# Second matmul of an MLP turned round: columns of D on the partitions, 512 tokens wide, results turned by DMA transposes

## Chip, cores, metric

One core of a Trainium2 chip. The metric is the device time of one execution in microseconds (us). All runs told here were in the fast state, except three of the four executions of x_act, which is said there; the medians are over four to six executions of a changed kernel and three to eleven of the kernel before.

## The reference

```python
B, S, D, F = 1, 2048, 1024, 3584          # x, w1, b1, w2, b2 in bf16
def reference(x, w1, b1, w2, b2):
    y = _layernorm(x, axis=-1)
    h = _gelu(jnp.einsum("bsd,df->bsf", y, w1) + b1)      # first matmul
    return jnp.einsum("bsf,fd->bsd", h, w2) + b2          # second matmul
```

## The kernel before

Both matmuls are done by the Strassen-Winograd scheme on two levels: an outer scheme of 7 products replaces 8, and each of these is again 7 inner products. VectorE forms the sums of inputs and outputs, ScalarE copies partial sums between PSUM and SBUF, TensorE does the products. In the code `p` is the outer product, `q` the inner one, `u, v` the quarter of the result, `dt` (after) a tile of 128 columns of D. In stage 2 the last outer product is `p = 3`.

The kernel plans itself while it is built: it gives every instruction a cost from a small table, schedules it, and places the buffers by a search with a random `SEED`. Its order of DMA issues thus depends on what it believes a DMA costs.

Before, h is the stationary operand. A product is 14 matmuls of 256 columns, tokens come out on the partitions, and a result needs one addition and one store:

```python
def finish(b, i, k, u, v, a, na, bb, nb, name, t0=0, nt=2, q="SP"):
    o = M.alloc(nt * 512, "o")
    ...
    op("DVE", 0.08 + n / 960, lambda e: e.tensor_tensor(out=v16(o, 0, 2 * n, BF16), in0=a, in1=bb, op=ALU.add),
       r=[na, nb], w=[o.c()], name=name, lat=D_PS_LAT)
    store(b, i, k, u, v, o, t0, nt, q)          # rows of 512 B straight to the output

def prod2(b, p):
    ...
            for t in ts:                        # two tiles of 128 tokens
                for k in range(KQ):             # KQ = 7
                    i = e.matmul(bank2(bank)[:, t, :], lhsT=av3[:, k, t * P:(t + 1) * P], rhs=bv[:, k, :], ...)

c_seq = [("c", b, p) for p in P_ORDER for b in range(NB)]     # the two token halves one after the other
```

## Time and profile before

| | before |
|---|---|
| median (range), 3 runs | 334.92 us (334.42 to 335.51) |
| span of the profiled execution | 332.0 us |
| first matmul of 512 columns / first matmul of stage 2 / last matmul ends | 16.26 / 177.05 / 329.43 us |
| tail, from the last matmul to the end | 2.57 us |

The span is what the core itself records; the time of the same execution is 1.7 us longer. I cut the span into four: head (up to 16.26), stage 1 (to 177.05), stage 2 (to 329.43), tail. Before, TensorE is busy without a gap in the middle two, and the chain, the groups and some stretches that show it stand in the prediction. From the view of busy time by stretches of the kernel before (stretch, then busy us and count of PE, weight loads, VectorE, ScalarE, GpSimd, then clock, DMA share, GB/s):

```profile
300.00:320.00 20.00, 20.00 (x186) 17.93 (x184) 16.37 (x24) 4.07 (x7) 0.00 (x0) 1.00 0.73 206
320.00:332.00 12.00, 9.42 (x87) 8.19 (x84) 6.30 (x10) 0.59 (x1) 0.00 (x0) 1.00 0.26 77
```

At the end each of the last two stores lands (its completion is signalled) 1.6 us after its issue, the last at 331.5. The span ends 0.5 us after that.

### The profile page before, as it was taken

What the parts mean: (1) busy time and instruction counts of PE and PEld (TensorE: products, weight loads), DVE (VectorE), ACT (ScalarE), POOL (GpSimd) and SP (SyncE); (2) the same over time, 40 slices, a digit from 0 to 9 for tenths busy, and PEclk for the clock granted to TensorE, in tenths of its full rate; (3) what the DMA queues carried; (4) which work ended last, traced back from release to release, by engine and by line L of the source; (5) the groups of instructions that cost most, each with busy time, mean ns of one, the idle gap of its engine ahead of it and who ended that gap; (6) DMA issues with size and microseconds to landing.
All of it is one profiled execution on the core that took longest, in us unless ns stands there. A gap on an engine that the chain in (4) does not pass through costs nothing.

```text
span 332.0 us, 6015 instructions
## 1 busy us (share of the span) xinstructions
PE 328.2 (99%) x2328; PEld 220.2 (66%) x2328; DVE 297.8 (90%) x483; ACT 180.3 (54%) x307; POOL 12.7 (4%) x28
## 2 busy tenths in 40 slices
PE   8999999999999999999999999999999999999996
PEld 5944444444444444444447888888888888888885
DVE  5989999999999969977889995899999999999935
ACT  4697999899676776767765555533021222222020
POOL 2210021002000000000000000000000000000000
PEclk9999999999999999999999999999999999999999
DMA  8996899999997999999949462654856547569732
GB/s 233 324 242 189 276 249 335 260 320 290 300 337 258 345 330 310 317 355 300 283 142 305 132 204 71 198 146 136 238 162 188 163 126 206 177 165 266 199 109 79
DMA packets 103622, 76.88 MB, mean 232 GB/s; under 512 B 16426, under 2 KB 94890, under 8 KB 103594
## 3 DMA queue, kind: packets, MB, share of 16 engines
q1 hardware_dynamic: 103034, 76.18, 78.2%
q8 instruction: 18, 0.29, 0.4%
q10 hardware_dynamic: 560, 0.33, 0.3%
q14 instruction: 10, 0.08, 0.1%
HBM read 48.96 MB, written 24.38 MB: 221 GB/s over the span
## 4 chain that ended last, share of the span: by engine, by line
PE 97%; DMA 2%; SPq 1%; DVE 0%; issue 0%
PE ps L908 49%; PE ps L1175 45%; PE ps L1238 2%; DMA mem<-in_w_dram 2%; PE ps L705 0%; SPq L644 0%; SPq L772 0%; DVE mem L1095 0%; SPq L641 0%; PE ps L1197 0%; PE ps L1250 0%
## 5 line engine op out<-in xcount | busy, mean ns | idle before, releaser
L908 PE MATMUL ps<-mem 128*128 128x512 f16 x756 | 164.0, 379 | 0.0
L1175 PE MATMUL ps<-mem 128*128 128x256 f16 (+1 forms) x1372 | 150.4, 273 | 0.0
L1175 PEld LDWEIGHTS ps<-mem 128*128 128x128 f16 x1372 | 134.2, 98 | 16.4
L908 PEld LDWEIGHTS ps<-mem 128*128 128x128 f16 (+1 forms) x756 | 73.7, 98 | 88.6 <-ACT mem L838 0.9
L838 ACT COPY mem<-ps 128x512 f32<-128x512 f32 x111 | 64.7, 588 | 76.6 <-PE ps L1175 59.3
L822 ACT ACTIVATE mem<-ps,b_sb 128x512 f16<-128x512 f32 x112 | 73.9, 692 | 21.4 <-PE ps L908 14.7
L846 DVE TENSOR_TENSOR ps<-ps,mem 128x512 f32<-128x512 f32 x84 | 58.4, 695 | 17.4 <-ACT mem L838 15.1
L1065 DVE TENSOR_TENSOR mem<-mem 128x1792 f16<-128x1792 f16 x56 | 60.1, 1085 | 3.5 <-PE ps L1175 2.7
L783 DVE TENSOR_TENSOR mem<-mem 128x1024 f16<-128x1024 bf16 (+1 forms) x56 | 37.8, 686 | 1.0 <-DMA mem<-in_w_dram 0.7
L974 DVE TENSOR_TENSOR mem<-mem 128x512 f16<-128x512 f16 (+5 forms) x84 | 37.4, 463 | 0.8 <-DMA mem<-in_w_dram 0.2
L1076 DVE TENSOR_TENSOR mem<-mem 128x1792 f16<-128x1792 f16 x32 | 33.8, 1085 | 0.1
L829 ACT COPY ps<-ps 128x512 f32<-128x512 f32 x31 | 17.7, 570 | 27.4 <-PE ps L1175 25.2
L1095 DVE TENSOR_TENSOR mem<-ps,mem 128x512 bf16<-128x512 f32 (+1 forms) x25 | 16.4, 666 | 2.2 <-PE ps L1175 2.0
L958 DVE TENSOR_TENSOR mem<-mem 128x2048 f16<-128x2048 bf16 (+1 forms) x16 | 17.4, 1087 | 0.1
L669 DVE BATCH_NORM_STATS2 st_sb<-mem 128x6 f32<-128x512 bf16 x22 | 14.2, 680 | 3.4 <-DMA mem<-in_x_dram 3.4
L1108 DVE TENSOR_TENSOR mem<-ps,mem 128x512 f32<-128x512 f32 x24 | 16.1, 684 | 0.0
L749 DVE TENSOR_TENSOR mem<-mem 128x512 f16<-128x512 f16 x32 | 11.9, 418 | 0.2
L675 POOL TENSOR_TENSOR rstd_sb<-vpe_sb,nhalf 128x1 f32<-128x1 f32 x11 | 6.6, 598 | 48.0 <-DVE vpe_sb L672 48.0
L1197 PE MATMUL ps<-ones 128*128 128x128 bf16 (+1 forms) x55 | 6.7, 287 | 1.1 <-POOL ones L610 1.1
L1238 PE MATMUL ps<-mem 128*128 128x128 f16 x112 | 7.4, 219 | 0.1
L678 DVE TENSOR_SCALAR mem<-mem,mv_sb,rstd_sb 128x1024 f16<-128x1024 bf16 (+1 forms) x12 | 6.1, 519 | 0.9 <-POOL rstd_sb L675 0.7
L651 ACT ACTIVATE mem<-mem 128x1024 f16<-128x1024 bf16 x5 | 5.3, 1069 | 2.8 <-DMA mem<-in_x_dram 2.8
(33 smaller groups left out, 62.5 us busy)
## 6 DMA issues: line engine op xcount, KB each, us to landing
mem<-in_w_dram SPq DMA_DIRECT2D x80, 256.0 KB, 5.0
mem<-w_scr SPq DMA_DIRECT2D x28, 448.0 KB, 3.7
w_scr<-mem SPq DMA_DIRECT2D x21, 512.0 KB, 5.5
w_raw<-mem SPq DMA_DIRECT2D x12, 512.0 KB, 5.0
mem<-w_raw SPq DMA_DIRECT2D x12, 448.0 KB, 4.3
mem<-in_w_dram SPq DMA_DIRECT2D x9, 448.0 KB, 4.5
mem<-in_x_dram SPq DMA_DIRECT2D x15, 256.0 KB, 4.1
out_dram<-mem SPq DMA_DIRECT2D x30, 128.0 KB, 3.2
```

What stands on the lines that cost most here:

```text
L783: op("DVE", d_tt(n), lambda e: e.tensor_tensor(out=o[0], in0=a[0], in1=bb[0], op=f), r=[a[1], bb[1]], w=[o[1]], name=f"w1S{k}_{ch}")
L822: op("ACT", A_GELU, lambda e: e.activation(out=dst, in_=bank2(bank), func=ACT.Gelu_apprx_tanh, bias=b1_sb[:, f:f + 1], scale=1.0), r=[bank ...
L829: op("ACT", A_CP, lambda e: e.copy(out=banks[dst][:, :], in_=banks[src][:, :]), r=[bank_c[src]], w=[bank_c[dst]], name=name, lat=A_LAT)
L838: op("ACT", A_CP, lambda e: e.copy(out=v16(a, 0, 2048, F32), in_=banks[src][:, :]), r=[bank_c[src]], w=[a.c()], name=name, lat=A_LAT)
L846: op("DVE", D_PS, lambda e: e.tensor_tensor(out=banks[dst][:, :], in0=banks[src][:, :], in1=v16(a, 0, 2048, F32), op=ALU.add), r=[bank_c[s ...
L908: i = e.matmul(banks[bank][:, :], lhsT=lv[:, k, :], rhs=rv[:, k, :], start=(fresh and k == 0), stop=(k == KH - 1), skip_group_check=True)
L958: op("DVE", d_tt(2 * self.n), lambda e: e.tensor_tensor(out=vd, in0=va, in1=vb, op=ALU.subtract), r=self.cells(a) + self.cells(bb), w=self ...
L974: tt = lambda o, a, c: (lambda e: e.tensor_tensor(out=o, in0=a, in1=c, op=ALU.subtract))
L1065: op("DVE", d_tt(UN // 2), lambda e: e.tensor_tensor(out=v16(t), in0=a[0], in1=bb[0], op=f), r=a[1] + bb[1], w=[t.c()], name=f"in{b}_{p}{q}")
L1076: op("DVE", d_tt(UN // 2), lambda e, va=va, vb=vb, vd=vd: e.tensor_tensor(out=vd, in0=va, in1=vb, op=f), r=h_cells(b, a, u, s) + h_cells(b ...
L1095: op("DVE", 0.08 + n / 960, lambda e: e.tensor_tensor(out=v16(o, 0, 2 * n, BF16), in0=a, in1=bb, op=ALU.add), r=[na, nb], w=[o.c()], name= ...
L1175: i = e.matmul(bank2(bank)[:, t, :], lhsT=av3[:, k, t * P:(t + 1) * P], rhs=bv[:, k, :], start=(fresh and t == ts[0] and k == 0), stop=(t ...
```

## The change

Intent: 512-column matmuls pay TensorE's fixed cost per instruction half as often. So w2 becomes the stationary operand, 512 tokens stream through, and D comes out on the partitions. The two column tiles run in lockstep, so that each w2 unit and each sum of inputs serves both. The price: a result has to be turned before it is stored. The core of the diff:

```diff
-            def finish(b, i, k, u, v, a, na, bb, nb, name, t0=0, nt=2, q="SP"):
+            def finish(dt, i, k, u, v, a, na, bb, nb, name, alone=False, q="SP"):
+                o = M.alloc(1024, "o")
+                wait = 1.0 if q == "ACTQ" else FIN_DUE
+                op("DVE", D_PS, lambda e: e.tensor_tensor(out=v16(o, 0, 1024, BF16), in0=a, in1=bb, op=ALU.add), ...)
+                view = v16(t, 0, 2048, BF16).rearrange("p (t c) -> p t c", t=4)   # t: one buffer for both column tiles
+                half = view[:, :, dt * P:(dt + 1) * P]
+                dma("SP", lambda e: e.dma_start_transpose(half, v16(o, 0, 1024, BF16)), [o.c()], [t.c(dt)], P * 1024 * 1.3, None, f"To{key}")
+                if alone:
+                    store(i, k, u, v, half, [t.c(dt)], dt * P, P, q=q)
+                elif len(t.cells) == 2:                                           # both tiles turned
+                    store(i, k, u, v, view, [t.c(0), t.c(1)], 0, 2 * P, q=q)
...
+                    # last two products: their partial sum, split in f16 hi and lo, is turned; the product comes out by tokens
+                    dma("SP", lambda e: e.dma_start_transpose(v3(tt, 0, 2048, 8), v16(hl)), [hl.c(0), hl.c(1)], [tt.c()], P * 2048 * 1.3, None, f"Td{n}")
...
-                        for t in ts:
-                            for k in range(KQ):
-                                i = e.matmul(bank2(bank)[:, t, :], lhsT=av3[:, k, t * P:(t + 1) * P], rhs=bv[:, k, :],
+                        for k in range(KQ):
+                            i = e.matmul(banks[bank][:, :], lhsT=bv[:, k, :], rhs=av3[:, k, :], ...)
...
-                        issue = 2.0 if t.name[:2] == "Td" else DMA_ISSUE
+                        issue = {"Td": 2.0, "To": 1.0}.get(t.name[:2], DMA_ISSUE)
-SEED = 12
+SEED = 4
+END_ORDER = "11 10 p41 p40 51 p31 61 50 p30 71 60 31 70 30 20 40 41 21"
```

The rest follows from it: sums of inputs cut at 4 + 3 slices, b2 loaded like b1 instead of broadcast. `END_ORDER` gives the last products by hand; its figures are inner product and column tile, `p` marks the outer product before the last.

## The prediction

> **What bounds the kernel now.** I read four views in this order: the chain of work that ended last, the costliest groups, the table of busy time by stretches, and the timeline of the end. The chain in order of time comes first, because it says whether anything but TensorE sets the span.
>
> ```profile
> 3.15 5.17 DMA mem<-in_w_dram
> ...
> 9.21 1.75 PE ps L1238 x28
> 10.96 0.61 PE ps L705 x8
> 11.57 1.56 PE ps L1238 x28
> ...
> 29.42 147.63 PE ps L908 x684
> 177.05 1.53 PE ps L1175 x14
> ...
> 185.76 143.68 PE ps L1175 x1316
> 329.43 0.02 issue
> 329.46 0.42 DVE mem L1095
> ```
>
> The columns are start, length and what ran. From 8.37 us (the first load of w1 has landed) to 329.43 us the chain is TensorE and nothing else. L908 is the first matmul, L1175 the second. Length over count gives the true spacing of one matmul, which the busy time of the groups does not: 147.63 / 684 = 0.2158 us for the 512-column matmuls of L908, 143.68 / 1316 = 0.1092 us for the 256-column ones of L1175, and 1.56 / 28 = 0.0557 us for the 128-column ones of L1238. So the span of 332.0 is a head of 8.37, TensorE for 321.06 without a gap worth naming, and a tail of 332.0 - 329.43 = 2.57 us.
>
> The groups show what the change acts on, and that the weight loads are not the bound:
>
> ```profile
> L908 PE MATMUL ps<-mem 128*128 128x512 f16 x756 | 164.0, 379 | 0.0
> L1175 PE MATMUL ps<-mem 128*128 128x256 f16 (+1 forms) x1372 | 150.4, 273 | 0.0
> L1175 PEld LDWEIGHTS ps<-mem 128*128 128x128 f16 x1372 | 134.2, 98 | 16.4
> ```
>
> A weight load lasts 98 ns and runs beside the matmul before it. The spacing of L1175 is 109 ns, so the load just fits, and no stretch of the second matmul waits for anything (idle 0.0).
>
> Then the stretches, because the second engine matters as soon as TensorE gets faster. The columns are stretch, length, busy us and count of PE, weight loads, VectorE, ScalarE and GpSimd, then clock, DMA share and GB/s:
>
> ```profile
> 200.00:220.00 20.00, 20.00 (x186) 17.92 (x184) 15.03 (x17) 10.07 (x18) 0.00 (x0) 1.00 0.54 151
> 220.00:240.00 20.00, 20.00 (x186) 17.94 (x184) 19.92 (x24) 5.26 (x9) 0.00 (x0) 1.00 0.55 163
> ...
> 280.00:300.00 20.00, 20.00 (x185) 17.91 (x184) 19.98 (x28) 4.08 (x7) 0.00 (x0) 1.00 0.65 183
> ```
>
> VectorE (19.92 of 20) looks as full as PE. It has looser ends: 15.03 in one stretch, and idle time from 317 us on. The clock is 1.00, so there is no throttle to win back. The DMA engines have about 40% free in this stage.
>
> **What the Trainium skill says.** (1) "TensorE: Matmul & The Clock Gate", the sections "Wait — 56ns, not 53.3ns?" and "Back-to-back issue gap": warm spacing is N / 2.4 ns plus a fixed 2.5 ns or so per matmul. That gives 215.8, 109.2 and 55.8 ns for 512, 256 and 128 columns, and the trace has 215.8, 109.2 and 55.7. The same page's sustained 131 ns for N = 512 does not hold here. So doubling the width saves one fixed 2.5 ns per pair and nothing else. (2) "DMA: Bandwidth & Descriptors", "DMA Transpose (X-bar)": the transpose takes 2-byte types only and must write to SBUF. That explains why a result is first rounded to bf16, turned, then stored, and why the last two partial sums, kept in f32, go as two f16 halves. The trace agrees as far as it goes: all 12 transposes of before are f16, SBUF to SBUF. (3) "Advanced Engine Details and Errata", "X-Bar Transpose (TRN2)": they are as fast as other DMAs. This trace says less than that: four of 256 KB issued back to back held the SP queue for 6.97 us, 1.74 each, with the DMA share at 1.07 to 1.42, which is some 150 GB/s. I use the trace. (4) "DMA: Bandwidth & Descriptors", "Specifications", asks for at least 512 B per transfer for line rate; no run here shows it yet. Most stores stay at 512 B rows, because two column tiles are gathered before storing; the last ones become 256 B rows.
>
> **The change, part by part.** *Matmuls.* Before: 7 outer by 7 inner products by 2 token halves = 98 products of 14 matmuls, 1372 in all: 1372 x 0.1092 = 149.8 us. After: also 98 products, for 2 column tiles instead of 2 token halves. 96 of them are 7 matmuls of 512 columns: 672 x 0.2158 = 145.0 us. The last two, which come out by tokens, are 28 matmuls of 128 columns each: 56 x 0.0557 = 3.1 us. Sum 148.2, so the chain gets **1.6 us shorter**. This is the only gain that I can find on the path, and nearly its ceiling. The weight loads fall from 1372 to 728. That is off the path, since they were hidden already.
>
> *VectorE.* The sums of inputs serve both column tiles: 28 pairs of 2048 and 1536 elements in place of 56 of 1792. From the rows 1219 ns at 2048 and 1085 at 1792, 1536 elements should take about 951, so a pair is 2170, exactly twice 1085. The outer sums go the same way. Additions into and out of PSUM keep their number and width. The turned pair adds about 5 operations of 0.69 us = 3.4 us, all in the last 25 us, where VectorE has idle time (6.30 busy of the last 12). Nothing lands on the path but in the tail.
>
> *ScalarE.* Saves, copies and bias seeds keep their number and their 0.59 us each. The order changes: with the two tiles in lockstep product 6 and product 7 of one group are one product apart (1.5 us) instead of two (3.1 us), and the save of PSUM lies between them. The next product would issue some 1.5 us after the last issue slot of the first; the save can start 0.16 us after that slot (379 ns duration less 216 spacing), lasts 0.59 and leaves about 0.7 us. One foreign copy of 0.59 ahead of it just fits. I allow 0.2 us of waits in all.
>
> *DMA.* New: 30 transposes of 128 KB and 2 of 256 KB. At 1.74 us per 256 KB that is 30 x 0.87 + 2 x 1.74 = 30 us of the SP queue and the DMA engines in 150 us, raising the share from about 0.58 to 0.78. Gone: the 256 KB broadcast of b2. Loads of w2 come once in two products evenly, instead of seven in a row and then none. They are let go five products ahead, 7.6 us, and land in 3.0 to 6.1 us, so a queue held for up to 1.5 us does no harm to the slowest. I allow 0.3 us.
>
> *Head.* b2 comes as one more small load like the one of b1, which held SP for 0.54 us amid the first loads. They feed PE closely (one wait of 0.3 us there). I allow 0.2 us.
>
> *Tail.* Before, the last lines are these (start, length, engine, line):
>
> ```profile
> 327.93 1.19 DVE L1095 TENSOR_TENSOR mem<-ps,mem 128x512 bf16<-128x512 f32 x2 [0.24 <-PE ps L1175]
> 329.46 0.42 DVE L1095 TENSOR_TENSOR mem<-ps,mem 128x256 bf16<-128x256 f32 x1 [0.34 <-PE ps L1175]
> ```
>
> A 256-wide addition of 0.42 and a 64 KB store of about 1.6 us end the kernel. After, the last product is by tokens and its second half again needs a 256-wide addition and a 64 KB store, now in 256 B rows: about +0.2. The last *turned* result competes with it. It ends two products, 1.5 + 1.6 = 3.1 us, before the end of PE; then addition 0.69, transpose to landing 2.6 to 3 (my estimate for half of those that took 3.1 at least), store about 2.2: 3.1 short of it plus 5.5 to 5.9 gives +2.4 to +2.8, plus issue times 0.2 to 0.5. Both paths are near 2.8 to 3.1 after the last matmul, against 2.57. I take +0.4 us.
>
> **Sum.** -1.6 + 0.2 + 0.3 + 0.2 + 0.4 = -0.5 us at cautious allowances, and -1.4 if only half of the tail's cost comes and nothing waits. I choose -1.1 us, nearer the good end, because the look-aheads and the order of the end are evidently set by hand to keep PE fed. 334.92 - 1.1 = 333.8 us.
>
> **Rivals.** (a) *VectorE becomes the bound.* For it: 80 us at over 99% busy, and both token halves of an outer sum now fall due at the same product, so the deadlines bunch. Against: the total is unchanged, it was idle 5 of 20 us in one stretch, and PE waited for VectorE nowhere. Busy time there also overlaps (two 1085 ns operations take 2.09 us), so its true load is nearer 95%. If it goes this way: 2 to 5 us of waits of PE on VectorE or on tiles that it writes, 336 to 339. (b) *The SP queue blocks.* A store behind its own transpose waits for the landing, 3 us or so, and a load of w2 may stand behind it. For it: SP already waited up to 4.0 us for VectorE before a store. Against: those waits cost PE nothing, the loads have 1.5 to 4.6 us to spare. If so: a few waits of 1 us each, 335 to 337; a bad order could cost over 7 us, which I count as the tail. (c) *The weight loads were the hidden bound* at 98 of 109 ns, and 512 columns free more than the fixed cost. Against: 109.2 is exactly what 2.4 GHz gives. If so, it would be some 330. (d) *The turned tail dominates:* landing of 4.2 us, the median of the large ones, gives +1.5 us, 334.9.
>
> **Range and chances.** The floor is a full 1.6 with an unchanged tail, 333.3, less the noise of three runs (334.42 to 335.51), hence 332.8. Rivals (b) and (d) together reach 336, my upper end. Over 2% faster means under 328.2, which no part of the sum can give. Over 2% slower means above 341.6, which needs a blocked queue many times over.
>
> **What would show it.** In the profile after: a chain still all PE from about 8.4 us to within 3 us of the end; 672 matmuls of 512 columns at 0.2158 us in the second stage; no PE idle time put down to VectorE, ScalarE or DMA over 0.5 us in sum; VectorE busy within 4 us of 297.85; DMA share about 0.78 in the second stage. I am wrong if PE shows gaps between products of the second stage (then the line named before the gap says which rival), or if the last store starts more than 2 us after the last matmul.

## The result, and the profile after

After: median 337.43 us (336.01 to 338.33, 6 runs), before in the same rounds 334.79 (334.33 to 335.51, 6 runs). The ratio is 1.0075, 95% interval 1.0051 to 1.0100. All ratios and intervals are from the runs of both kernels in the same rounds, so not quite the ratio of the medians. The prediction was wrong in its sign: it had 1.1 us less than before, and the medians are 2.6 us apart the other way.

The profiled execution is the slowest of the six; its span is 336.6, 4.6 us more than before, whose profiled execution was in turn a quick one. So differences of the two profiles are larger than that of the medians. Here is its chain in order of time:

```profile
89.32 5.16 DMA mem<-in_w_dram
94.51 0.70 DVE mem L782
95.25 83.05 PE ps L921 x384
178.31 1.51 PE ps L1242 x7
...
304.74 5.71 DMA mem<-w_raw
310.50 16.79 PE ps L1242 x77
327.29 3.14 PE ps L1249 x56
330.45 0.42 DVE mem L1209
```

The first matmul is L921 now, the second L1242, its part by tokens L1249. Three things differ from before. In stage 1 PE's weight loads waited twice for a sum of w1 (L782), 1.5 us in all, before 82.58 and 95.25; the second time the load of w1, issued at 89.32, had landed late. A load of w2 at 304.74 landed late. And the last matmul ends at 330.43, while the span goes on to 336.6: a tail of 6.17 us instead of 2.57. Cut as above:

| part | before | after | difference |
|---|---|---|---|
| head, to the first 512-column matmul | 16.26 | 16.50 | +0.24 |
| stage 1 | 160.79 | 161.81 | +1.02 |
| stage 2 | 152.38 | 152.12 | -0.26 |
| tail | 2.57 | 6.17 | +3.60 |

The groups of the second matmul:

```profile
L1242 PE MATMUL ps<-mem 128*128 128x512 f16 x672 | 145.9, 379 | 1.2 <-DMA mem<-w_raw 1.2
L1242 PEld LDWEIGHTS ps<-mem 128*128 128x128 f16 (+1 forms) x672 | 65.7, 98 | 80.7 <-DMA mem<-w_raw 1.7
```

PE waited in stage 2 once, 1.2 us for that load of w2. Weight loads fell to half; x_direct shows below that this brings nothing of its own. Most of the loss is the tail. Its timeline (start, length, engine, line, then what the engine waited for):

```profile
324.77 1.49 SPq L1191 DMA_TRANSPOSE mem<-mem  x1
...
326.30 5.29 SPq L1120 DMA_TRANSPOSE mem<-mem  x4
...
327.33 0.69 DVE L1111 TENSOR_TENSOR mem<-ps,mem 128x512 bf16<-128x512 f32 x1 [0.22 <-PE ps L1242]
...
328.88 5.57 ACTq L1100 DMA_DIRECT2D out_dram<-mem  x6
```

The last turned result is ready at 327.33 + 0.69 = 328.02. Four transposes stand in the SP queue from 326.30 to 331.59, one behind the other; the last is issued at 330.3, so this result stood in the queue for 2.3 us. It lands 3.7 us later; its store is the last of the six at ACT's queue (the line ends at 334.45), issued at 334.1 and landing 2.0 us later, at 336.1. The span ends 0.5 us after that, as before. The other path to the end is late too: the store of the last product by tokens, ready at 330.87, stands behind the same four transposes, goes out at 331.64 and lands at 334.9, so that the tail would be some 5 us even without the turned result. The stretches show what the transfers met:

```profile
280.00:300.00 20.00, 20.00 (x94) 9.11 (x93) 18.60 (x26) 4.07 (x7) 0.00 (x0) 1.00 1.04 213
300.00:320.00 20.00, 18.82 (x88) 8.34 (x86) 17.13 (x26) 4.33 (x8) 0.00 (x0) 1.00 1.11 264
320.00:336.60 16.60, 10.41 (x90) 6.31 (x88) 8.80 (x15) 1.56 (x3) 0.00 (x0) 0.89 1.05 194
```

The DMA share is 1.04 to 1.11 over the last 55 us, against 0.65, 0.73 and 0.26 before. I had averaged the new load over all of stage 2.

### The profile page after: what moved, and what is told of

Same layout as the page of the kernel before. It is cut to its first block, busy times and chain, and to the rows that moved or that the text cites. A ratio compares the mean times of both kernels' runs of the same rounds, so it can differ in the third digit from the quotient of the medians.

```text
span 336.6 us, 4741 instructions
## 1 busy us (share of the span) xinstructions
PE 327.4 (97%) x1684; PEld 154.7 (46%) x1684; DVE 299.7 (89%) x488; ACT 181.1 (54%) x309; POOL 14.1 (4%) x28
## 3 DMA queue, kind: packets, MB, share of 16 engines
q10 hardware_dynamic: 3056, 1.11, 1.4%
## 4 chain that ended last, share of the span: by engine, by line
PE 88%; DMA 5%; ACT 2%; SPq 1%; DVE 1%; issue 0%; POOLq 0%; POOL 0%
PE ps L921 43%; PE ps L1242 42%; DMA mem<-in_w_dram 3%; PE ps L1315 2%; DMA mem<-w_raw 2%; PE ps L1249 1%; ACT mem L653 1%; ACT mem L826 1%; DVE mem L782 1%; SPq L771 1%; POOLq L571 0%; ACT mem L842 0%; PE ps L704 0%; SPq L643 0%; ACT mem L650 0%
## 5 line engine op out<-in xcount | busy, mean ns | idle before, releaser
L921 PE MATMUL ps<-mem 128*128 128x512 f16 x756 | 164.3, 379 | 0.5 <-DVE mem L782 0.4
L1242 PE MATMUL ps<-mem 128*128 128x512 f16 x672 | 145.9, 379 | 1.2 <-DMA mem<-w_raw 1.2
L921 PEld LDWEIGHTS ps<-mem 128*128 128x128 f16 (+1 forms) x756 | 73.4, 98 | 90.5 <-DVE mem L782 1.5
L1242 PEld LDWEIGHTS ps<-mem 128*128 128x128 f16 (+1 forms) x672 | 65.7, 98 | 80.7 <-DMA mem<-w_raw 1.7
L1078 DVE TENSOR_TENSOR mem<-mem 128x2048 f16<-128x2048 f16 (+1 forms) x56 | 59.6, 1087 | 2.1 <-PE ps L1242 1.6
L782 DVE TENSOR_TENSOR mem<-mem 128x1024 f16<-128x1024 bf16 (+1 forms) x56 | 37.9, 688 | 2.8 <-DMA mem<-in_w_dram 2.4
L1090 DVE TENSOR_TENSOR mem<-mem 128x2048 f16<-128x2048 f16 (+1 forms) x32 | 33.4, 1089 | 0.0
L1111 DVE TENSOR_TENSOR mem<-ps,mem 128x512 bf16<-128x512 f32 x22 | 15.0, 688 | 3.3 <-PE ps L1242 3.2
L1228 ACT COPY ps<-b_sb 128x512 f32<-128x512 f32 x6 | 3.5, 590 | 7.4 <-DVE mem L1139 7.2
```

The lines of the kernel that those rows point to most:

```text
L782: op("DVE", d_tt(n), lambda e: e.tensor_tensor(out=o[0], in0=a[0], in1=bb[0], op=f), r=[a[1], bb[1]], w=[o[1]], name=f"w1S{k}_{ch}")
L921: i = e.matmul(banks[bank][:, :], lhsT=lv[:, k, :], rhs=rv[:, k, :], start=(fresh and k == 0), stop=(k == KH - 1), skip_group_check=True)
L1078: op("DVE", d_tt((k1 - k0) * 512), lambda e, a=a, bb=bb, o=o: e.tensor_tensor(out=o, in0=a[0], in1=bb[0], op=f), r=a[1] + bb[1], w=[t.c(z) ...
L1090: op("DVE", d_tt((k1 - k0) * 512), lambda e, va=va, vb=vb, vd=vd: e.tensor_tensor(out=vd, in0=va, in1=vb, op=f), r=h_cells(b, a, s, k0, k1 ...
L1242: i = e.matmul(banks[bank][:, :], lhsT=bv[:, k, :], rhs=av3[:, k, :], start=(fresh and k == 0), stop=(k == KQ - 1), skip_group_check=True)
```

## The experiments

Theory T: the loss is the hop through a transpose, which costs the issuing queue a fixed time per instruction, and which bunches at the end. Rivals: B, any extra hop (a transfer SBUF to SBUF between the sum and its store) would do the same (it is the store behind a landing, not the transpose); P, the placement and order that the kernel's planner found are bad, or its cost table misleads it; S, the SP queue alone is at fault, another queue would cure it. The expectations use letters in a sense of their own, which each of them gives. Kernels that give a wrong result are marked; all others were correct.

### x_plain: transposes become plain copies of the same bytes (wrong result)

```diff
-dma("SP", lambda e: e.dma_start_transpose(half, v16(o, 0, 1024, BF16)), ...)
+dma("SP", lambda e: e.dma_start(half, v16(o, 0, 1024, BF16).rearrange("p (t c) -> p t c", t=4)), ...)
```

The two pairs of 256 KB likewise; same plan.

> The changed kernel with each of the 32 DMA transposes replaced by a plain SBUF-to-SBUF copy of the same bytes, in the same place of the same queue (result wrong on purpose). Plan, order and semaphores are the same. Theory T (a transpose holds the SP queue 1.24 us whatever its size and the last ones pile up): the tail after the last matmul falls from 6.2 us to 3.5 or less, the wait of 1.2 us for w2 near 305 us goes, time 333.5 to 335. Rival R1 (it is the extra step, SBUF to SBUF and then to memory, with its two landings in a row, not the kind of transfer): the tail stays over 5 us and the time within 1 us of 337.4. Rival R2 (the first stage is what lost): the first second-stage matmul starts again near 178.3 us against 177.05 before, and most of the loss stays.

Measured 335.02 us, ratio 1.0010 (0.9985 to 1.0036), span 333.4. No PE wait in stage 2, tail 4.75. Neither expectation of the tail came true (3.5 or less, or over 5): of the 3.6 us by which it had grown, 2.2 remain with a copy, and 1.4 are due to the kind of transfer. With copies no result stands in the SP queue: the last one is issued within 0.1 us and lands 2.3 us later, at 328.6. But its store is the last of six in ScalarE's queue and goes out only at 330.0, so a part of what remains is the order of the stores.

### x_direct: no hop at all (wrong result)

The 30 results are stored as they come, unturned, in rows of 256 B; the two turned pairs stay.

```diff
-dma("SP", lambda e: e.dma_start_transpose(half, v16(o, 0, 1024, BF16)), ...)
+store(i, k, u, v, v16(o, 0, 1024, BF16).rearrange("p (t c) -> p t c", t=4), [o.c()], dt * P, P, q=q)
```

> The changed kernel without turning: each sum is stored straight from the result tile, in 256-byte rows (result wrong on purpose); the two turned pairs of partial sums at the end stay. Theory T: second stage without a PE wait, 672 matmuls at 0.2158 us and 56 at 0.0557, so about 1.6 us shorter than before's 152.4 from its first second-stage matmul to the last; tail 2.5 to 3.5 us; time 333.3 to 334.8 (the upper end if the first stage's 1.0 us of waits returns). Rival R2 (first stage or wider matmuls cost it): 336 or more.

Measured 333.11 us, ratio 0.9964 (0.9932 to 0.9995). The edit also adds one dependency, so that two reads of one PSUM bank by ScalarE and VectorE have an order in the new plan; x_pair, x_plan, x_end, x_split and x_seed16b carry it too. The end of its chain (the second matmul is L1230 and L1237 here):

```profile
184.59 140.51 PE ps L1230 x651
325.10 3.14 PE ps L1237 x56
328.24 0.02 issue
328.26 0.42 DVE mem L1197
```

Stage 2 runs from 177.47 to 328.24, 150.77 us, 1.61 less than before, which is the prediction's -1.6 to the digit. The tail is 330.8 - 328.24 = 2.56, as before. So the matmul side of the change does what was promised, and half as many weight loads bring nothing beyond it. The loss in stage 2 and in the tail is in getting the results turned.

### x_late and x_early: which of the transposes

x_late makes the 8 transposes of the last outer product copies, x_early the other 24 (both give a wrong result; same plan):

```diff
# x_late
-e.dma_start_transpose(half, src)
+e.dma_start(half, src) if name[3] == "3" else e.dma_start_transpose(half, src)
# x_early
+e.dma_start_transpose(half, src) if name[3] == "3" else e.dma_start(half, src)
```

(`src` abbreviates the view of `o`; in x_late the two pairs are copies too.)

> Plan and order of the changed kernel; only the 8 transposes of the last outer product (6 results, 2 pairs of partial sums) become plain copies of the same bytes (result wrong on purpose); the 24 before stay. Theory P (the end is lost to the last transposes queueing behind each other): tail after the last matmul falls from 6.2 to 4.5 to 5 us, as with all of them plain (4.8), time 335.3 to 336.5, the wait for w2 near 305 us stays. Rival B (a backlog of the transposes before holds the end back): tail stays at 6 or more.

> The complement: the 24 earlier transposes become plain copies (result wrong on purpose), the last 8 stay. Theory P: the tail stays at 5.5 to 6.5 us and the wait for w2 near 305 us goes; time 335.5 to 337. Rival B: tail 4.5 to 5 us, and waits of PE stay where they were.

x_late 335.42 us, ratio 1.0028 (1.0012 to 1.0045), tail 4.78. x_early 336.12, ratio 1.0063 (1.0040 to 1.0086), tail 5.25. Against x_plain (1.0010, in other rounds) the 24 early transposes add 0.0018, the 8 late ones 0.0053: 0.6 and 1.8 us of 334.3. The intervals of neighbours overlap (x_plain and x_late, x_late and x_early), and the 1.8 us are not all the late transposes' doing: in its profile PE waited 0.9 us in stage 1, before any result is turned, where x_plain had 0.1. The tails are the better measure: 4.75 with copies only, 4.78 with the 24 early transposes, 5.25 with the 8 late ones, 6.17 and 6.36 (x_again) with both. So the late ones alone add 0.5, the early ones alone nothing, and both together 1.4 to 1.6; the two don't simply add. The last turned result stood in the SP queue for 0.0, 0.0, 1.4 and 2.3 to 2.4 us in these four cases: the late ones make the queue, and the early ones put it a further 0.9 us behind. The expectation for x_early (tail 5.5 to 6.5 us) was thus missed. The timeline of x_early has the same row in its tail as the changed kernel:

```profile
324.18 5.31 SPq L1120 DMA_TRANSPOSE mem<-mem  x4
```

and that of x_plain, with copies:

```profile
323.09 3.78 SPq L1120 DMA_DIRECT2D mem<-mem  x4
```

The wait for w2 near 304 us comes with the early transposes: it is there in x_late, not in x_early.

### x_pair and x_split: larger and smaller transposes

x_pair gathers both column tiles and turns them by one transpose of 256 KB (14 of these and 2 of 128 KB). x_split cuts each of 128 KB into two of 64 KB:

```diff
# x_split
-dma("SP", lambda e: e.dma_start_transpose(half, v16(o, 0, 1024, BF16)), ...)
+for z in range(2):
+    dma("SP", lambda e, z=z: e.dma_start_transpose(half[:, 2 * z:2 * z + 2, :], v16(o, 512 * z, 512, BF16)), ...)
```

> Both column tiles of a quadrant are gathered in one tile and turned by one transpose of 256 KB, so 30 transposes of 128 KB become 14 of 256 KB and 2 of 128 KB; result right. Theory T (fixed 1.24 us or so each on the queue): SP spends about 18 us less on transposes, at most one or two stand in the queue at the end, tail 3 to 4 us, time 334 to 335.5. Rival R3 (the cost of a transpose goes with its bytes, on the DMA engines): issue of the 256 KB ones 1.7 us and more, tail over 5 us, time 336.5 to 338.

> Each transpose of 128 KB is cut into two of 64 KB, same bytes; result right. Theory T (a transpose holds the queue 1.2 us whatever its size): issue stays at 1.1 to 1.25 us each, SP spends 35 us more, PE waits for w2 several times, time 341 or more. Rival R3 (by bytes): issue about 0.6 us, time within 1.5 us of the changed kernel.

x_pair 338.64 us, ratio 1.0125 (1.0091 to 1.0160). x_split 360.48 us, ratio 1.0781 (1.0743 to 1.0820). The time for which one issue held the queue (min/median/max ns, first and last start), in the changed kernel, x_plain, x_split and x_pair in turn:

```profile
L1120 SPq DMA_TRANSPOSE mem<-mem x30: 1188/1237/1953, 231.6 to 330.3; - x30
```

```profile
L1120 SPq DMA_DIRECT2D mem<-mem x30: 593/605/920, 231.1 to 326.3; - x30
```

```profile
L1121 SPq DMA_TRANSPOSE mem<-mem x60: 1167/1244/2368, 231.1 to 348.9; - x60
```

```profile
L1135 SPq DMA_TRANSPOSE mem<-mem x14: 1237/1278/3007, 233.9 to 325.0; - x14
```

A transpose holds its queue for 1.24 us at 64 KB (x_split), 1.24 at 128 KB and 1.28 at 256 KB (medians); a copy of 128 KB for 0.605. Between these sizes the cost is per instruction. About 1.2 us is a floor: the maxima are 2 to 3 us, and the 12 transposes of 256 KB in the kernel before, in a stage with DMA shares of 1.02 and 1.03, have the same minimum and a higher median:

```profile
L731 SPq DMA_TRANSPOSE mem<-mem x12: 1238/1608/2802, 17.8 to 83.5; - x12
```

Twice as many (x_split) cost 24 us against x_again of the same rounds. About 8 of these are in stage 2, where PE waited nine times, 6.4 us in all, six times for w2. The other 16 are in the tail, 22.5 us long: SP still has transposes and stores to issue until 354, 18 us after the last matmul. The DMA share was 0.64 to 0.72 over the last 58 us, well below the 1.05 of the changed kernel, so here the queue is the limit and not the engines:

```profile
320.00:340.00 20.00, 13.56 (x102) 7.11 (x99) 10.27 (x17) 2.79 (x5) 0.00 (x0) 0.98 0.64 142
340.00:358.70 18.70, 0.00 (x0) 0.00 (x0) 1.45 (x3) 0.00 (x0) 0.00 (x0) 0.50 0.72 172
```

Half as many (x_pair) did not help, against the expectation of T: no wait for w2 was left, but the tail was 8.3 us. A 256 KB transpose can only go when both tiles are done, so the turned partial sum of the last products went out at 326.38, behind two of these, and VectorE waited 2.7 us for it.

### x_act: another queue

```diff
-dma("SP", lambda e: e.dma_start_transpose(...
+dma("ACTQ", lambda e: e.dma_start_transpose(...
```

> All 32 transposes issued from the ScalarE queue instead of SP; result right. If the SP queue is what loses the middle (loads of w2 behind transposes and stores): no PE wait for w2. Rival S: ScalarE is in order as well, so its saves of PSUM come late and PE waits for ScalarE 1 to 4 us. The tail stays over 5 us under both, since the last transposes still stand in one queue; time 335.5 to 338.5.

Far worse: 344.82 us in the one fast execution, against 334.14 before; the other three (350.25 to 350.95) were slow, and there is no ratio. In the profile of the fast one ScalarE's saves of PSUM came late behind the transposes in its own queue, and PE waited for them twice, 2.2 us in all. Waits for w2 did not go, as they should have if the transposes in the SP queue were their only cause: three, 2.0 us. The tail was 8.4. So another queue is no cure, and the document's rival S falls: the cost moves with the transposes.

### x_plan, x_seed12, x_seed16b: the planner

x_plan gives the planner figures nearer to the measured ones (issue 1.0 to 1.3 us, transfer 0.47 to 1.27 us); x_seed12 takes the placement seed of the kernel before, x_seed16b seed 16, which the planner itself rates best.

```diff
# x_plan
-issue = {"Td": 2.0, "To": 1.0}
+issue = {"Td": 2.0, "To": 1.3}
-..., P * 1024 * 1.3, None, f"To{key}")
+..., P * 1024 * 3.5, None, f"To{key}")
# x_seed12, x_seed16b
-SEED = 4
+SEED = 12        # 16
```

> Only the planner's estimate of a 128 KB transpose is changed (issue 1.0 to 1.3 us, transfer 0.47 to 1.27 us), so that stores no longer stand in the queue before their transpose has landed. Theory T: the middle wait for w2 (1.2 us) goes, since it came from a store that held the queue; the end stays, because as many transposes are due there; tail 5 to 6.5 us, time 336 to 337. Rival R2: the time moves by less than 0.5 us and the waits of the second stage stay.

> The changed kernel with the seed of the kernel before for the placement in memory; result right. Theory L (the 1.0 us lost in the first stage comes of the placement and the order planned from it, not of the change): the first stage moves by 0.5 to 2 us either way, the tail stays over 5 us; time 336 to 339. Rival: first stage and time within 0.5 us of the changed kernel's.

> The changed kernel with placement seed 16 (the best of 40 by its own plan) and an explicit order for the two reads of one PSUM bank that this placement left open; result right. Theory L: first stage 147.6 to 148.2 us long, tail still 5.5 us or more, time 335.8 to 337. Rival (placement alone makes the change pay): under 334.5.

x_plan 339.35 us, ratio 1.0134 (1.0101 to 1.0167): stage 1 got longer (stage 2 began at 179.58), the wait for w2 shrank to 0.2 us, at 326, the tail stayed at 6.8. x_seed12 345.3, ratio 1.0331 (1.0281 to 1.0380): PE waited 5.5 to 6.0 us for w1 in stage 1 and stage 2 began at 186.06. x_seed16b 340.33, ratio 1.0171 (1.0141 to 1.0202). The tails of the last two were 7.6 and 8.1, and the times expected were missed by all three. A first build with seed 16 was REFUSED for unordered reads of a PSUM bank, as told at x_direct; the changed kernel's own seed happens to order them. So placement alone moves the time by up to 8 us, and the seed of the change is the best of the three that ran. Rival P holds in that the plan matters; it does not explain the tail, which is 6 us and more in every plan with all transposes kept.

### x_again: the changed kernel once more

> The changed kernel once more, for a second profile of it on another chip. If what the first profile showed is the kernel's own: tail after the last matmul 5.5 to 6.5 us, one wait for w2 of about 1 us near 305 us, first stage 0 to 1.2 us longer than 147.6; time 336 to 338. If the first profile was an outlier: tail under 4.5 us.

336.59 us, ratio 1.0062 (1.0038 to 1.0086), on another chip. The tail recurs (6.36), and so does the wait for w2. Its chain shows how that comes about:

```profile
299.41 3.63 DMA mem<-mem
...
303.05 0.38 SPq L1100
...
303.47 5.49 DMA mem<-w_raw
```

A transpose lands at 303.04; the store of what it turned (L1100), standing in the same queue, goes only then; the load of w2 stands behind the store and lands at 308.96, just too late (PE idle 0.2 us here, 1.2 in the first profile). The 684 matmuls that make up most of stage 1 took 147.78 us where the kernel before took 147.63, so of its +1.0 in the first profile most was not there this time.

### x_end: the last results straight out (wrong result)

Only the six single results of the last outer product are stored unturned; 24 transposes and the two pairs stay.

```diff
+if q == "ACTQ":
+    store(i, k, u, v, v16(o, 0, 1024, BF16).rearrange("p (t c) -> p t c", t=4), [o.c()], dt * P, P, q=q)
+    return
```

> Only the six turned results of the last outer product are stored straight, without a transpose (result wrong on purpose); the 24 transposes before stay, and so do the 2 turned pairs. Theory E (nearly all of the tail is the extra hop of the last results): tail 2.5 to 3.2 us; time 334 to 336, depending on the wait for w2 near 305 us, which may stay. Rival B (backlog of earlier transposes and stores): tail over 4 us.

336.1 us, ratio 1.0053 (1.0029 to 1.0077). The new plan lost more in stage 1 (stage 2 began at 179.20), and the end was still late, with a tail of 4.2 us: VectorE waited for the turned pair, from the chain

```profile
324.38 5.54 DMA mem<-mem
```

which landed at 329.9. I had expected a tail like before (2.5 to 3.2 us); over 4 was what the rival of this run said, a backlog of earlier transposes and stores. With the six gone, the next transpose in line sets the end: it is the last turned thing, whatever it is, that counts.

### Tries at a version that beats both

x_tok24 and x_tok10 let the last six products come out by tokens, so that no result is turned behind the last matmul, and turn their partial sums early, as single f16 (seed 24 with the old cost table, seed 10 with the measured one; edits of some 100 lines). x_pairtok19 and x_pairtok4 also pair the two column tiles, so that 16 transposes of 256 KB remain. Their order of the end:

```diff
-END_ORDER = "11 10 p41 p40 51 p31 61 50 p30 71 60 31 70 30 20 40 41 21"
+END_ORDER = "11 10 p41 p40 51 p31 50 61 p30 60 71 70 31 21 41 30 40 20"   # x_tok24, x_tok10
+END_ORDER = "11 10 p41 p40 51 50 p31 p30 61 60 71 70 21 20 31 30 41 40"   # x_pairtok19, x_pairtok4
```

> Result right. The last six products of the last outer product all come out by tokens, their partial sums turned early as one f16 half (128 KB each), so no transpose lies behind the last four products; b2 is loaded from the ScalarE queue; placement seed 24, the best of 80 by the kernel's own plan. Theory Q (the tail is lost to transposes that start after the last sums): tail 2.5 to 3.2 us instead of 6.2, time 333.8 to 335.5 (matmuls cost 0.2 us more than in the changed kernel). Rival: the DMA engines are full through the last 30 us, so PE waits or late landings eat it: tail over 4 us or PE waits over 1.5 us, time 336 or more.

> As the run before, but planned with the measured figures of a transpose (1.3 us of the queue, 0.87 us of transfer) and seed 10, the best of 60. Theory Q: tail 2.5 to 3.2 us, fewer waits for w2 than the run before, time 333.8 to 335.5. Rival: the plan with longer transposes pushes other work and loses 1 to 3 us in the first stage, as the earlier run with corrected figures did: 336 to 338.

> Result right. All results and all partial sums of the last outer product turned in pairs, 16 transposes of 256 KB in place of 32; the last six products come out by tokens. The plan's old figures for a transpose, seed 19 (best of 40 by the plan). Theory T (a transpose holds the queue 1.24 us whatever its size, and the loss is where they bunch): SP spends about 20 us on them in place of 40, PE waits for w2 under 0.5 us in all, tail 2.5 to 3.3 us, time 333.3 to 335. Rival V (the bytes turned in the last third are the limit): DMA share over 1.0 from 300 us, tail or PE waits over 3 us more, 336 or more.

> The same with the measured figures of a transpose in the plan (1.3 us of the queue, 1.46 us of transfer for 256 KB) and seed 4. Theory T: as above, 333.3 to 335. Rival V: 336 or more.

x_tok24 341.19 us, ratio 1.0206 (1.0177 to 1.0235); x_tok10 339.05, 1.0134 (1.0112 to 1.0156). x_pairtok19 336.71, 1.0067 (1.0049 to 1.0084); x_pairtok4 337.04, 1.0086 (1.0066 to 1.0106). None beats the kernel before, and none reached the tail expected (2.5 to 3.3 us): in the same order the tails are 7.5, 7.8, 6.2 and 6.7. The DMA share in x_pairtok19 was 1.03 and 1.11 from 300 us on, as its rival V had it; V is not excluded. In x_pairtok19 stage 1 and stage 2 run without any wait of PE; what is left is the tail, in its chain:

```profile
319.15 5.38 PE ps L1270 x97
324.52 6.10 DMA mem<-mem
...
330.72 0.69 DVE mem L1227
```

and at the SP queue, in its timeline:

```profile
321.25 3.18 SPq L1136 DMA_TRANSPOSE mem<-mem  x2
...
324.52 2.13 SPq L1206 DMA_TRANSPOSE mem<-mem  x1
```

The last partial sum's transpose (L1206) stands behind two transposes of results (L1136) and lands 6.1 us after its issue, at 330.62, two us after the last matmul. An order that lets it go first was not run, so whether such a version comes under the kernel before is open; the results' own transposes, now behind it, would still have to land and be stored.

## Why the prediction was wrong, point by point

- **Matmuls, -1.6 us: right.** x_direct has stage 2 shorter by 1.61 us. It is the only gain, as said. (The parts as printed, 145.0 and 3.1, add up to 148.1, not 148.2.)
- **VectorE, nothing: right.** Busy 299.7 us against 297.85, within the 4 us allowed; 1221 ns at 2048 elements and 953 at 1536, and no wait of PE on VectorE in stage 2. Rival (a) fell. Rival (c) fell as well: weight loads went from 66% to 46% of the span, with no gain beyond the 1.6.
- **Waits of ScalarE and DMA, 0.2 + 0.3: right in sum or somewhat low.** One wait for w2, 1.2 us in the first profile and 0.2 in x_again, by just the way that rival (b) described: a store behind its own transpose, a load behind the store. None for ScalarE.
- **Head, +0.2: right in the first profile** (+0.24), low in x_again (+0.64). Stage 1 was not in the sum at all: +1.0 in one profile, +0.15 in the other. That the new placement of buffers is behind this is not shown, but x_seed12 shows that placement could have cost 8 us.
- **Tail, +0.4: this step failed.** It measured +3.6 and +3.8 in the two profiles. Put into the sum in place of 0.4, 3.6 gives -1.6 + 0.2 + 0.3 + 0.2 + 3.6 = +2.7 us; the ratio is worth +2.5 (that it comes so near is partly luck, since the tail is from profiles, which differ by 4.6 and 3.3 us). The mechanism, rival (d), was named and its way was followed rightly: addition, transpose, landing, store. After the last matmul of 512 columns, which ends 3.1 us before the end of PE as I had it, the profile has 0.7 for the addition, 2.3 in the SP queue, 3.7 to the landing, 2.0 to the landing of the store and 0.5 to the end of the span; less the 3.1 that is the tail of 6.17 but for rounding. The terms were mis-sized:
  - I took the transpose at 0.87 us of the queue, half of a 256 KB one by its bytes. It is about 1.2 us at least and 1.24 to 1.28 in the median, at 64 as at 256 KB (x_split, x_pair). The trace of before already spoke against halving: the four back to back, 1.74 on average, were one of 2.8 and three of 1.3 to 1.4, and the minimum of the twelve is 1.24.
  - I let it meet an empty queue, with "issue times 0.2 to 0.5". It stood for 2.3 us behind others, the largest single error. The last outer product ends all its results within a few us, so their transposes bunch: with these 8 alone the wait is 1.4 us (x_early), with the other 24 as well 2.3; with copies in their place it is 0.0 (x_plain).
  - I took a landing of 2.6 to 3 us and a store of 2.2. They were 3.7 and 2.0. The 0.5 us from the last landing to the end of the span, which the kernel before has too, I left out on this path. The DMA share at the end is 1.05, not the average of the stage, which I had right (0.78 expected, 0.80 measured); that the landing is slow because of it is argued and not shown. No transpose of a result starts before 231.6 us, so their 30 us of DMA work, which I had about right in sum (28.8 us more in the changed kernel than in x_direct, from shares by lengths), fell into 105 us instead of 150.
- **B against T: both hold in part.** With copies in place of transposes the time is 1.0010 of before, with no hop 0.9964: the second hop alone costs 0.0046, 1.5 us (in the profiles 2.2 us of tail), and takes back nearly all of the matmuls' gain. That transposes are slower than copies is the rest, 2.2 us (1.4 to 1.6 of it in the tail). I had the hop in the working, but ended it at the same moment as the other path to the end instead of behind it.
- **What would show it.** Both signs of being wrong that I had named came: a gap of PE between products of stage 2, and a last store long after the last matmul (3.6 us, with 2 as the limit). On a reading: the trace shows the 12 transposes of before as SBUF to SBUF and gives no type; that they are f16 is from the kernel's text.

Why the planner's own order of the end is so unforgiving is only argued: its cost table lets a transpose hold the queue for 1.0 us and the engines for 0.47 us, where 1.24 was measured and 0.96 is my estimate (last section). The larger figures did not mend it (x_plan), so something else in the plan has its part, and that stays open.

## What to carry to other kernels

A saving per instruction has a ceiling that can be worked out before anything is built (count times fixed cost, here 1.6 us); weigh it against every step that is added behind the last result, because each of those counts in full at the end. For new transfers, look at when they fall and behind what they stand, not at the average load of the stage, and count instructions, not bytes, for the queue that issues them. If the last of a chain of results is taken out, the next one sets the end: the whole bunch must move, and with a self-planning kernel each such move also draws a new placement that can cost more than what is at stake.

## What the Trainium skill lacked or had wrong

- "Advanced Engine Details and Errata", "X-Bar Transpose (TRN2)", has transposes as fast as regular DMAs. Here SBUF to SBUF at 128 KB they held the issuing queue for 1.24 us against 0.605 for a plain copy, and the whole kernel was 2.2 us slower with transposes than with copies of the same bytes.
- No page that I found gives, measured on trn2 and for several sizes, the time for which one transpose holds its queue: here 1.244, 1.237 and 1.278 us (medians) at 64, 128 and 256 KB, and 1.6 us at 256 KB in the busy first stage of the kernel before, with a minimum of 1.24.
- "DMA: Bandwidth & Descriptors", "Latency and other measured facts", gives 261 GB/s as the effective rate of a transpose with a non-contiguous middle dimension, 350 to 400 when contiguous. My estimate from the DMA shares here is 28.8 us for 30 transposes of 128 KB, 0.96 each, some 136 GB/s, beside other traffic.
- "TensorE: Matmul & The Clock Gate", "Back-to-back issue gap": its sustained 81 ns at 128 columns and 131 ns at 512 did not hold. The trace has 215.8 ns at 512, 109.2 at 256, 55.7 at 128; the same page's N / 2.4 ns plus 2.5 ns holds for all three.
